# Evacuation order on ScalarE in two steps of nine, and a semaphore tie for the zeroing and the first weight loads, in an attention and routed-experts kernel

## The chip, the cores and the metric

The kernel runs on one core of one Trainium2 chip. The metric is the device time of one execution in microseconds (us). The kernel before was run three times: median 999.24 us, from 998.72 to 999.63. One further execution was profiled; every row quoted below is from that execution.

## What is computed

Attention over 8 batches of 8 heads, 576 positions of 64 values each, with a threshold: a score counts only where it lies within tau of its row's maximum. The output, 4608 rows of 512 values, goes through a layer of eight experts; each row goes to the one expert with the largest logit.

```python
scores = scale * np.matmul(q, k.transpose(0, 1, 3, 2))
thresh = np.max(scores, axis=-1, keepdims=True) - tau
scores = np.where(scores >= thresh, scores, -1000000000.0)
attn = np.exp(scores - np.max(scores, axis=-1, keepdims=True))
attn = attn / (np.sum(attn, axis=-1, keepdims=True) + 1e-09)
x = (attn @ v)                      # then (4608, 512)
logits = x @ w_gate
e_idx = np.argmax(logits, axis=1)
...
for e in range(E):
    mask = e_idx == e
    h = np.maximum(x[mask] @ w1[e], 0.0)
    out[mask] = gate_w[mask, None] * eom[mask, e, None] * (h @ w2[e])
```

## The kernel before

**Attention.** A unit `u` is one head of two batches; there are 32 units, taken two at a time: 16 pairs `m`. A pair has nine steps `s` (0 to 8), so the loop in `run` (L306) counts steps `g = 9 m + s` from 0 to 143. A step handles 128 query rows of both batches (step 4 of a pair takes the last 64 rows of both of its units). In a step, TensorE first writes the scores into the two `ps` tiles (L138). VectorE copies them out, negated and scaled, as `s`, with the row minimum in `mn` (L146). GpSimd adds tau: `thr` (L151). This instruction is kept as `router.gate`, so `gate` is always the threshold of the newest step. ScalarE takes the exponentials into `p` (L158, two instructions of 128x576). One step later VectorE sets to zero in `p` what misses the threshold and sums the rest (L171). Two steps later TensorE transposes `p` in 64x64 blocks into the tile `pt` (L213) and ScalarE copies `pt` into `PTa` or `PTb` (L216). There is one `pt` buffer, so the transposes of the next step wait for this copy. The product with v follows (L235, into `pa`), some of its matmuls in eight of the nine steps; `X` is its result (L240).

**Steps with rows.** In steps 1 and 5 of every pair from the second on (`ROWS`, L29), TensorE also turns the result of an earlier unit back into rows of x and multiplies them with the two gate matrices (L261). In these steps `p`'s remainder goes through the same two PSUM tiles (L197), and ScalarE copies `xl` (L327) and the remainder (L198) out of them. Then stand, on ScalarE, the exponentials of the step (L332) and behind them the copy of the blocks (L334, which calls `blocks`).

**A transfer on ScalarE's queue.** At the end of each odd unit, ScalarE issues a copy of `PTc` into `PTb` (L218), which L235 reads three steps later. As every transfer of the two hardware queues, it is given one of eight completion semaphores (lanes) in turn, whichever engine issues it, and before it is issued the engine waits until the earlier transfer of the same lane has landed.

**Routing.** From step 10 on, 32 transfers of 128 rows each (L446) write the same tile `zrow` to the buffer of routed rows `xs` in device memory; one is emitted per step. Later, rows of x are scattered into `xs` on GpSimd's queue (L461), with a wait for all 32 and for the gate of their step.

**Loads.** SyncE issues all other transfers: q and k of a unit (L92) and v (L97), two units ahead, and the experts' weights in pieces of 512 KB (L707 and L708). `begin` (L765) is called in step 129 and emits the first eight of these. For ScalarE, VectorE, TensorE and GpSimd the instructions stand in the order in which the program is written. SyncE's order is set by a scheduler: an instruction of SyncE is placed as early as the things that it depends on allow.

**Experts.** From about step 146 on, TensorE multiplies gathered rows with the weights (L927 to L929, L949 to L951), each number split into a high and a low part, and scaled rows are scattered into the output (L740).

Of the kernel before, what the change touches and what calls it, by code (L numbers as in the profile page):

```python
# [16 lines left out]
P = 128  # L17
# [3 lines left out]
class Attention:  # L21
# [279 lines left out]
    def run(self, hooks):  # L301
        nc, T, G, rt = self.nc, self.T, self.G, self.router
        W, NB = self.XW, self.NB
        st, pr, av, xls = {}, {}, {}, {}
        self.prep_first()
        for g in range(G + self.TAIL):  # L306
            m, s = divmod(g, T)
            if g < G:
                u, t = self.at(g)
                if t == 0 and u + 2 < self.nu:  # L310
                    self.load_qk(u + 2)
                    self.load_v(u + 2)
                st[g] = self.scores(u, t)
            if g in self.WARM:
                self.keep_warm(self.WARM[g])
            g2 = g - 2
            turn = 0 <= g2 < G
            if turn:
                dst = self.turned(*self.at(g2))
            xu = 2 * m + self.ROWS[s] if m and s in self.ROWS else None  # L320
            if xu is not None:
                ps = self.x_rows(xu)
                if turn:
                    out = self.remainder(dst, pr[g2], [x[:, 5 * W : 5 * W + 64] for x in ps])
                xl = xls[xu] = self.w2.tile([P, 2, 5, W], F32, name="xl")
                for a in (1, 0):
                    nc.scalar.copy(xl[:, a].rearrange("p j w -> p (j w)"), ps[a][:, 0 : 5 * W])  # L327
                    if turn:
                        out(a)
                self.x_out(xu, xl)  # L330
            if g < G:
                pr[g] = self.exps(u, t, *st[g])  # L332
            if turn and xu is not None:
                self.blocks(dst, pr.pop(g2))  # L334
            if s in self.AV:
                du, n = self.AV[s]
                au = 2 * m + du
                if 0 <= au < self.nu:
                    if au not in av:
                        av[au] = self.av_units(au)  # L340
                    for _ in range(n):
                        next(av[au])
            if turn and xu is None:
                p = pr.pop(g2)
                self.remainder(dst, p)
                u2, t2 = self.at(g2)
                self.blocks(dst, p, u2 % 2 and t2 == 2)
            if s in self.PLACE:
                rt.place(self.ps_r)
            g1 = g - 1  # L350
            if 0 <= g1 < G:
                self.masks(*self.at(g1), *st.pop(g1), pr[g1])
            lu = 2 * m + self.LOGITS[s] if m and s in self.LOGITS else None
            if g >= G:
                lu = xu
            if lu is not None and lu in xls:
                self.logits(lu, xls.pop(lu))
                if lu == self.nu - 1:
                    self.logit_sums(0)
                    self.logit_sums(1)  # L360
            if self.sumup and s in self.ROUTE:
                self.logit_sums(self.summed)
            if g in hooks:
                hooks[g]()
            rt.advance(s in self.ROUTE or m >= self.nu // 2 - 5)


class Router:
# [69 lines left out]
    def init_units(self):  # L438
        E = self.E
        parts = [(self.xs[self.A :, :], "itok")]  # L440
        for e in range(self.early, E + 1):
            n = self.base[e] if e < E else 2 * P
            parts.append((self.xs[e * self.CAP : e * self.CAP + n, :], "itok"))
        for dst, group in parts:
            for r in range(0, dst.shape[0], P):
                ins = self.nc.sync.dma_start(dst[r : r + P, :], self.zrow)  # L446
                self.nodep(ins, group)
                self.init.append(ins)
                yield False

# [216 lines left out]
class Experts:  # L667
# [26 lines left out]
        for name, bufs in (("y", 4), ("x", 2), ("h", 2)):  # L694
            setattr(self, f"ps_{name}", self.pool(f"ps_{name}", bufs, space=PSUM))

    def load(self, e, g):
        nc = self.nc
        r1 = self.raw.tile([P, 4, 256], F32, name="r1")
        r2 = self.raw.tile([P, 2, 512], F32, name="r2")  # L700
        cs = slice(g * 256, g * 256 + 256)
        if isinstance(e, int):
            s1, s2 = self.w1[e, :, cs], self.w2[e, cs, :]
        else:
            s1, s2 = self.w1[bass.ds(e, 1), :, cs], self.w2[bass.ds(e, 1), cs, :]
            s1, s2 = (s.rearrange("o d f -> (o d) f") for s in (s1, s2))
        nc.sync.dma_start(r1, s1.rearrange("(c p) f -> p c f", p=P))  # L707
        nc.sync.dma_start(r2, s2.rearrange("(c p) f -> p c f", p=P))  # L708
        return r1, r2

    def split_w(self, raw):
# [79 lines left out]
    def load_next(self):  # L791
        if self.nload < len(self.seq):
            i, g = self.seq[self.nload]
            self.nload += 1
            self.raws.append(self.load(self.unit(i).e, g))

    def split_until(self, n):
        while self.done < min(n, 2 * len(self.seq)):
# [345 lines left out]
```

## Time and profile before

| | |
|---|---|
| median of three runs | 999.24 us |
| the profiled execution, its own time | 1000.01 us |
| its span (first to last instruction) | 998.2 us |
| mean granted TensorE clock | 0.991 |
| busy TensorE, VectorE, ScalarE, GpSimd | 957.4, 691.0, 595.1, 347.2 us |
| moved by the transfer engines | 130.88 MB |

The span is 1.8 us shorter than the profiled execution's own time. The page cuts the span into 40 slices of 25 us; a digit is the busy share of a slice in tenths. In the list of waits, a row names the instruction that waited, then what released it, then microseconds in total, how often, and the longest. In a timeline, a row has the start, the duration, engine, line, what is written and read, and in brackets the idle time ahead of it with what ended it; rows that follow each other are merged, with their count. A row with `SPq` or `ACTq` is the issue of a transfer by that engine's queue, not the transfer.

### The profile page before, as it was taken

The numbers are of one execution on the slowest core, as the hardware profiler recorded it, in microseconds if no ns is written. First come the engines' busy times: TensorE is split into PE (matmuls) and PEld (weight loads), VectorE is DVE, ScalarE is ACT, GpSimd is POOL, SyncE is SP. The second block draws the span as 40 slices with busy tenths as digits, with TensorE's granted clock in tenths as the row PEclk, the third lists the DMA queues.
The fourth block names the chain that finished last, engine by engine and source line by source line (L and its number), as shares of the span: only waits on it lengthen the run. The fifth ranks groups of instructions, "written<-read, shape, count | busy, mean of one in ns | idle before, by whom it ended". The sixth has DMA issues, their size and how long they took to land. (4 is left out here: it accounts for less than half of the span.)

```text
span 998.2 us, 22132 instructions
## 1 busy us (share of the span) xinstructions
PE 957.4 (96%) x8491; PEld 715.0 (72%) x8491; DVE 691.0 (69%) x1632; ACT 595.1 (60%) x1052; POOL 347.2 (35%) x649
## 2 busy tenths in 40 slices
PE   9689999999999999999998999999999999999997
PEld 5456666666666666666667887788888878878785
DVE  7579989998899988998986675434634635535731
ACT  6478887877888778887884433333534424425621
POOL 4234343446844468454764821010102002002011
PEclk9799999999999999999999999999999999999999
DMA  9952222222432215223135775254644636527401
GB/s 270 309 176 87 75 67 88 59 73 58 158 95 58 88 51 164 86 64 86 61 98 180 243 244 179 86 168 127 202 154 142 215 100 209 182 85 234 157 21 44
DMA packets 87532, 130.88 MB, mean 131 GB/s; under 512 B 24831, under 2 KB 51711, under 8 KB 87424
## 3 DMA queue, kind: packets, MB, share of 16 engines
q1 hardware_dynamic: 62096, 103.70, 33.7%
q0 software_dynamic: 6640, 21.02, 5.5%
q10 hardware_dynamic: 18688, 4.72, 1.9%
q8 instruction: 68, 1.11, 0.5%
q14 instruction: 40, 0.33, 0.1%
HBM read 95.26 MB, written 30.22 MB: 126 GB/s over the span
## 5 line engine op out<-in xcount | busy, mean ns | idle before, releaser
L158 ACT ACTIVATE p<-s,mn 128x576 f32<-128x576 f32 x288 | 210.3, 783 | 65.4 <-DVE s L146 64.2
L146 DVE TENSOR_SCALAR_CACHE_REDUCE s<-ps 128x576 f32<-128x576 f32 x288 | 206.2, 753 | 43.1 <-PE ps L138 42.6
L171 DVE SCALAR_TENSOR_TENSOR p<-s,thr,p 128x576 f32<-128x576 f32 x288 | 224.8, 817 | 5.6 <-POOL thr L151 5.6
L138 PE MATMUL ps<-qk 64*128 64x288 f32 (+1 forms) x1280 | 182.6, 421 | 0.9 <-DVE s L146 0.6
L151 POOL TENSOR_SCALAR thr<-mn,tau_sb 128x2 f32<-128x2 f32 x144 | 99.4, 690 | 220.0 <-DVE s L146 217.9
L932 ACT ACTIVATE hh<-ph 128x512 fp32r<-128x512 f32 (+2 forms) x96 | 49.0, 511 | 201.9 <-PE ph L929 201.7
L740 POOL DMA_INDIRECT out_dram<-yo,kid x39 | 42.7, 1095 | 362.0 <-DVE yo L739 272.4
L933 DVE SCALAR_TENSOR_TENSOR hl<-ph,hh 128x512 fp32r<-128x512 f32 (+2 forms) x96 | 55.5, 578 | 136.6 <-ACT hh L932 136.6
L927 PE MATMUL ph<-xh,w1h 128*128 128x512 f32 (+2 forms) x384 | 135.9, 354 | 0.7 <-ACT xl L327 0.7
L928 PE MATMUL ph<-xl,w1h 128*128 128x512 f32 (+2 forms) x384 | 133.4, 347 | 0.2 <-DVE xl L752 0.2
L929 PE MATMUL ph<-xh,w1l 128*128 128x512 f32 (+2 forms) x384 | 133.2, 347 | 0.0
L138 PEld LDWEIGHTS ps<-qk 64*128 64x128 f32 (+1 forms) x1280 | 105.4, 178 | 27.3 <-DVE s L146 4.8
L951 PE MATMUL py<-w2h,hl 128*128 128x512 f32 x304 | 120.5, 396 | 1.2 <-DVE hl L933 1.2
L949 PE MATMUL py<-w2h,hh 128*128 128x512 f32 x304 | 120.2, 395 | 0.0
L950 PE MATMUL py<-w2l,hh 128*128 128x512 f32 x304 | 119.9, 394 | 0.0
L213 PE MATMUL pt<-ident,p 64*128 64x64 f32 x2304 | 101.2, 228 | 9.5 <-ACT PTb L216 9.5
L213 PEld LDWEIGHTS pt<-ident,p 64*128 64x128 f32 x2304 | 83.0, 138 | 30.3 <-issue 13.9
L235 PE MATMUL pa<-PTb,vld 128*64 128x320 f32 x640 | 101.1, 445 | 2.8 <-DMA PTb<-PTc 2.8
L235 PE MATMUL pa<-PTa,vld 128*64 128x256 f32 x640 | 83.9, 392 | 12.9 <-ACT PTb L198 12.9
L927 PEld LDWEIGHTS ph<-xh,w1h 128*128 128x128 f32 x384 | 72.1, 188 | 11.9 <-ACT xl L327 0.8
L928 PEld LDWEIGHTS ph<-xl,w1h 128*128 128x128 f32 x384 | 72.2, 188 | 10.2 <-DVE xl L752 0.6
L752 DVE TENSOR_TENSOR w1l<-r,w1h 128x1024 fp32r<-128x1024 f32 x52 | 64.0, 1230 | 21.5 <-ACT w1h L749 20.5
(203 smaller groups left out, 1501.3 us busy)
## 6 DMA issues: line engine op xcount, KB each, us to landing
r<-in_moe_w_dram SPq DMA_DIRECT2D x104, 512.0 KB, 3.9
qk<-in_qkv_dram SPq DMA_DIRECT2D x31, 608.0 KB, 4.1
vld<-in_qkv_dram SPq DMA_DIRECT2D x32, 320.0 KB, 4.0
xs<-zrow SPq DMA_DIRECT2D x32, 257.0 KB, 7.8
xg<-xs SPq DMA_DIRECT2D x6, 1028.0 KB, 5.4
PTb<-PTc ACTq DMA_DIRECT2D x16, 288.0 KB, 3.4
xg<-xs SPq DMA_DIRECT2D x4, 514.0 KB, 5.2
xg<-xs SPq DMA_DIRECT2D x2, 771.0 KB, 4.7
```

Source lines behind the costliest of these rows:

```text
L138: nc.tensor.matmul(ps[a][rows, o : o + HS], q[pp, t * P : t * P + w], k[pp, k0 : k0 + HS], start=True, stop=True)
L146: nc.vector.tensor_scalar(s, ps[a][:, c0 : c0 + S], SC, None, op0=ALU.mult, op1=ALU.min, accum_out=mn[:, a : a + 1])
L158: self.nc.scalar.activation(e, s, AF.Exp, bias=mn[:, a : a + 1], scale=-1.0)
L171: nc.vector.scalar_tensor_tensor(e, s, thr[:, a : a + 1], e, op0=ALU.is_le, op1=ALU.mult, accum_out=acc[:, a : a + 1])
L213: nc.tensor.transpose(pt[:, o : o + 64], p[hs[h], k0 : k0 + P], id_[hs[h], hs[h]])
L235: nc.tensor.matmul(pa[self.half[a], 0:N], vm[:, kb, a], PT[:, 4 * a + kb if i else self.NK - 1], start=(i == 0), stop=(i == self.NB), skip ...
L927: nc.tensor.matmul(ph, w1h[:, c, fs], self.xh[:, c, 0:N], start=(c == 0), stop=False)
L928: nc.tensor.matmul(ph, w1h[:, c, fs], self.xl[:, c, 0:N], start=False, stop=False)
L929: nc.tensor.matmul(ph, w1l[:, c, fs], self.xh[:, c, 0:N], start=False, stop=(c == 3))
L949: nc.tensor.matmul(Y, hh[:, ts], wh, start=(f == 0), stop=False)
L950: nc.tensor.matmul(Y, hh[:, ts], wl, start=False, stop=False)
L951: nc.tensor.matmul(Y, hl[:, ts], wh, start=False, stop=(f == 7))
```

## The change

Three edits. In `run`, the call of `blocks` in the steps with rows stands ahead of the exponentials. In `init_units`, each of the 32 zero writes waits for the threshold of the step that emits it. In `load`, the first eight weight loads wait for the threshold of the step that emits them, 129.

```diff
@@ run
                 self.x_out(xu, xl)
+            if turn and xu is not None:
+                self.blocks(dst, pr.pop(g2))
             if g < G:
                 pr[g] = self.exps(u, t, *st[g])
-            if turn and xu is not None:
-                self.blocks(dst, pr.pop(g2))
             if s in self.AV:
@@ init_units
                 ins = self.nc.sync.dma_start(dst[r : r + P, :], self.zrow)
                 self.nodep(ins, group)
+                self.after(ins, [self.gate])
                 self.init.append(ins)
@@ Experts.load
-    def load(self, e, g):
+    def load(self, e, g, gate=None):
...
-        nc.sync.dma_start(r1, s1.rearrange("(c p) f -> p c f", p=P))
-        nc.sync.dma_start(r2, s2.rearrange("(c p) f -> p c f", p=P))
+        for r, s in ((r1, s1), (r2, s2)):
+            ins = nc.sync.dma_start(r, s.rearrange("(c p) f -> p c f", p=P))
+            if gate is not None:
+                self.rt.after(ins, [gate])
         return r1, r2
@@ load_next
-            self.raws.append(self.load(self.unit(i).e, g))
+            self.raws.append(self.load(self.unit(i).e, g, self.rt.gate if self.nload <= self.RB else None))
```

On TensorE, VectorE and GpSimd no instruction moves. On ScalarE two rows change places in each step with rows. This is ScalarE's order in steps 1 and 2 of the second pair, before:

```order
L327 COPY xl<-pa 128x400
L198 COPY PTb<-pa 128x64
L327 COPY xl<-pr 128x400
L198 COPY PTb<-pr 128x64
L158 ACTIVATE p<-s,mn 128x576 x2
L216 COPY PTb<-pt 128x8x128
L158 ACTIVATE p<-s,mn 128x576 x2
```

and now:

```order
L327 COPY xl<-pa 128x400
L198 COPY PTb<-pa 128x64
L327 COPY xl<-pr 128x400
L198 COPY PTb<-pr 128x64
L216 COPY PTb<-pt 128x8x128
L158 ACTIVATE p<-s,mn 128x576 x4
L240 COPY X_206<-pa 128x256
```

The copy of `pt` has moved ahead of the step's two exponentials, which now stand directly ahead of those of the next step. The 30 steps with rows of the pairs from the second on all change in this way.

SyncE's queue near the start of the program, before (`qk_406` belongs to unit 3, `qk_595` and `vld_597` to unit 4; `r1_7321` and `r2_7322` are the first weights):

```order
L97 DMA vld_408<-in_qkv_dram 128x640
L446 DMA xs_71<-zrow_139 128x514 x9
L92 DMA qk_406<-in_qkv_dram 128x1216
L446 DMA xs_71<-zrow_139 128x514 x17
L92 DMA qk_595<-in_qkv_dram 128x1216
L446 DMA xs_71<-zrow_139 128x514 x5
L97 DMA vld_597<-in_qkv_dram 128x640
L446 DMA xs_71<-zrow_139 128x514
L707 DMA r1_7321<-in_moe_w1_dram 128x4x256
L708 DMA r2_7322<-in_moe_w2_dram 128x2x512
```

and now (`qk_868` and `vld_870` belong to unit 5, `qk_1081` to unit 6):

```order
L97 DMA vld_408<-in_qkv_dram 128x640
L92 DMA qk_406<-in_qkv_dram 128x1216
L92 DMA qk_595<-in_qkv_dram 128x1216
L97 DMA vld_597<-in_qkv_dram 128x640
L446 DMA xs_71<-zrow_139 128x514 x3
L92 DMA qk_868<-in_qkv_dram 128x1216
L446 DMA xs_71<-zrow_139 128x514
L97 DMA vld_870<-in_qkv_dram 128x640
L446 DMA xs_71<-zrow_139 128x514 x3
L92 DMA qk_1081<-in_qkv_dram 128x1216
L446 DMA xs_71<-zrow_139 128x514 x2
```

The zero writes now stand in groups of one to three between the loads of units 4 to 12, and every one of them waits for its own step. The first `PTc` copy of ScalarE gets another lane by this: before, its lane was last used by the 27th zero write (the first of the group of five above); now by the load of unit 1's q and k at the program's start.

SyncE's queue at the end of attention, before, held the loads of the last units (`qk_7393` and `vld_7395` are unit 31's) with nothing between them:

```order
L92 DMA qk_7081<-in_qkv_dram 128x1216
L97 DMA vld_7083<-in_qkv_dram 128x640
L92 DMA qk_7393<-in_qkv_dram 128x1216
L97 DMA vld_7395<-in_qkv_dram 128x640
L892 DMA xg_8127<-xs_71 128x3x514
```

and now (line numbers of the changed kernel, in which L709 is the weight load):

```order
L92 DMA qk_7081<-in_qkv_dram 128x1216
L97 DMA vld_7083<-in_qkv_dram 128x640
L709 DMA r1_7321<-in_moe_w1_dram 128x4x256
L709 DMA r2_7322<-in_moe_w2_dram 128x2x512
L709 DMA r1_7325<-in_moe_w1_dram 128x4x256
L709 DMA r2_7326<-in_moe_w2_dram 128x2x512
L709 DMA r1_7329<-in_moe_w1_dram 128x4x256
L709 DMA r2_7330<-in_moe_w2_dram 128x2x512
L709 DMA r1_7333<-in_moe_w1_dram 128x4x256
L709 DMA r2_7334<-in_moe_w2_dram 128x2x512
L92 DMA qk_7393<-in_qkv_dram 128x1216
L97 DMA vld_7395<-in_qkv_dram 128x640
```

The eight weight loads, 4 MB, have moved past the loads of 26 units and stand ahead of the last unit's.

## The prediction

> **What bounds the kernel now.** I read the page first: busy time by engine and in 40 slices.
>
> ```profile
> span 998.2 us, 22132 instructions
> PE 957.4 (96%) x8491; PEld 715.0 (72%) x8491; DVE 691.0 (69%) x1632; ACT 595.1 (60%) x1052; POOL 347.2 (35%) x649
> PE   9689999999999999999998999999999999999997
> PEclk9799999999999999999999999999999999999999
> DMA  9952222222432215223135775254644636527401
> ```
>
> TensorE (PE) is busy 96% of the span and in nearly every slice; it sets the end. It idles 998.2 - 957.4 = 40.8 us. Only the second and third slice (25 to 75 us) break the row: busy falls to 6 and 8 tenths, the granted clock to 7 in the second, just where the transfer engines are full. The list of waits says what TensorE stands for:
>
> ```profile
> PE pa L235 <- ACT PTb L198: 12.9, 16, 8.5
> PE pt L213 <- ACT PTb L216: 9.5, 15, 0.6
> PE pa L235 <- DMA PTb<-PTc: 2.8, 1, 2.8
> PE pr L526 <- ACT PTa L205: 1.3, 3, 0.5
> ```
>
> So there are two different things: one hole of 8.5 us with a smaller one of 2.8, and a wait of 0.6 us that comes back 15 times, once for each of the 15 pairs that have steps with rows. The rest of the first row, 12.9 - 8.5 = 4.4 us, is a wait for the remainder's copy (L198), which the change leaves in front as it was.
>
> **The hole.** TensorE's timeline around it, with the next two pairs (an L197 row marks step 1 of a pair at 35.94, 81.14 and 111.94):
>
> ```profile
> 35.94 0.22 PE L197 MATMUL pr<-ident,p 64*128 64x64 f32 x1
> 45.19 1.97 PE L235 MATMUL pa<-PTa,vld 128*64 128x256 f32 x8 [8.54 <-ACT PTb L198]
> 55.30 2.11 PE L235 MATMUL pa<-PTb,vld 128*64 128x320 f32 x8 [2.81 <-DMA PTb<-PTc]
> 81.14 0.22 PE L197 MATMUL pr<-ident,p 64*128 64x64 f32 x1
> 82.11 1.08 PE L235 MATMUL pa<-PTa,vld 128*64 128x256 f32 x8 [0.26 <-ACT PTb L198]
> 111.94 0.22 PE L197 MATMUL pr<-ident,p 64*128 64x64 f32 x1
> 118.44 1.30 PE L235 MATMUL pa<-PTb,vld 128*64 128x320 f32 x8
> ```
>
> ScalarE and its queue at the same time, then SyncE's queue, then the landing times:
>
> ```profile
> 43.81 0.68 ACTq L218 DMA_DIRECT2D PTb<-PTc  x1
> 44.53 0.49 ACT L327 COPY xl<-pa 128x400 f32<-128x400 f32 x1 [9.47 <-DMA xs<-zrow]
> 110.11 0.60 ACTq L218 DMA_DIRECT2D PTb<-PTc  x1
> ```
>
> ```profile
> 35.45 4.75 SPq L446 DMA_DIRECT2D xs<-zrow  x5
> 42.23 0.43 SPq L707 DMA_DIRECT2D r<-in_moe_w_dram  x1
> 50.24 2.12 SPq L708 DMA_DIRECT2D r<-in_moe_w_dram  x1
> ```
>
> ```profile
> xs<-zrow SPq DMA_DIRECT2D x32, 257.0 KB, 7.8
> PTb<-PTc ACTq DMA_DIRECT2D x16, 288.0 KB, 3.4
> qk<-in_qkv_dram SPq DMA_DIRECT2D x31, 608.0 KB, 4.1
> ```
>
> ScalarE had nothing to wait for from TensorE, yet stood 9.47 us, and a zero write ended that. Ahead of L327 on its queue is the issue of the `PTc` copy, which must wait for its lane. The lane's last user is the first zero write issued at 35.45; with the median landing of 7.8 it is done at 43.25, and the issue follows at 43.81. Behind the issue stand the copies that free `pa`, and so TensorE stands. Then the `PTc` copy itself travels among the last zero writes and the weight loads of 42 to 52 us: it is used 55.30 - 43.81 = 11.5 us after its issue, against a median landing of 3.4. That is the second hole.
>
> **Part one: zero writes and weights move away.** The interval from step 1 to step 1 is 81.14 - 35.94 = 45.20 us with the holes and 111.94 - 81.14 = 30.80 without. The difference, 14.40, is 8.54 + 2.81 of idle and 3.05 of slower matmuls behind them: eight L235 took 1.97 instead of 1.08, and 2.11 instead of 1.30.
>
> By the Trainium skill ("TensorE: Matmul & The Clock Gate", section "What's actually happening") the array falls to half its clock only after an idle window of about 3.4 us and is back after as long of work. An estimate from that page gives 8.54 + 2.81 + 1.7 = 13.05, since a gap of 2.81 would cost no clock; the 2.11 behind that gap speaks against it here.
>
> I take 14.4. The `PTc` copy's lane was now last used by a load from the first microseconds, so its issue does not wait. Where do the moved transfers collide now? The zero writes come one in a step, behind `thr`. On SyncE's queue the loads of q, k and v stand behind them, and whoever reads those waits on TensorE. Two rows show the spare time; 90.94 is unit 7's load and 120.52 the first scores that read it:
>
> ```profile
> 90.94 0.33 SPq L92 DMA_DIRECT2D qk<-in_qkv_dram  x1
> 120.52 1.20 PE L138 MATMUL ps<-qk 64*64 64x288 f32 x16
> 469.88 0.33 SPq L92 DMA_DIRECT2D qk<-in_qkv_dram  x1
> 499.58 0.71 PE L138 MATMUL ps<-qk 64*64 64x288 f32 x8
> ```
>
> 120.52 - 90.94 - 4.1 = 25.5 us to spare; a gate holds a load back by a step at most (30.80 / 9 = 3.4). The eight weight loads took about 10 us (42.23 to 52.36) and now stand ahead of unit 31's loads, which have 499.58 - 469.88 - 4.1 = 25.6 us to spare. Both cost nothing; without that cover, a weight burst ahead of a load costs its 10 us once. In GpSimd's queue nothing moves; the scatters are emitted after the last zero write, as before.
>
> **Part two: the copy ahead of the exponentials.** Steps 5 and 6 of an ordinary pair on ScalarE, TensorE and VectorE:
>
> ```profile
> 96.77 1.47 ACT L158 ACTIVATE p<-s,mn 128x576 f32<-128x576 f32 x2
> 98.12 1.03 ACT L216 COPY PTb<-pt 128x1024 f32<-128x1024 f32 x1
> 99.01 1.48 ACT L158 ACTIVATE p<-s,mn 128x576 f32<-128x576 f32 x2
> ```
>
> ```profile
> 98.17 0.39 PE L202 MATMUL pr<-ident,p 128*64 128x128 f32 x4
> 99.20 0.71 PE L213 MATMUL pt<-ident,p 64*128 64x64 f32 x16 [0.64 <-ACT PTb L216]
> 99.74 1.19 PE L138 MATMUL ps<-qk 64*128 64x288 f32 x8
> ```
>
> ```profile
> 98.12 0.75 DVE L146 TENSOR_SCALAR_CACHE_REDUCE s<-ps 128x576 f32<-128x576 f32 x1
> 98.80 0.81 DVE L171 SCALAR_TENSOR_TENSOR p<-s,thr,p 128x576 f32<-128x576 f32 x1
> 99.54 0.87 DVE L171 SCALAR_TENSOR_TENSOR p<-s,thr,p 128x576 f32<-128x576 f32 x1
> 100.97 0.76 DVE L146 TENSOR_SCALAR_CACHE_REDUCE s<-ps 128x576 f32<-128x576 f32 x1 [0.55 <-PE ps L138]
> 446.27 0.76 DVE L146 TENSOR_SCALAR_CACHE_REDUCE s<-ps 128x576 f32<-128x576 f32 x1 [0.34 <-PE ps L138]
> ```
>
> TensorE could go on at 98.17 + 0.39 = 98.56 but `pt` is being copied until 99.15. With the copy first, from 96.77 to 97.80, `pt` is free 0.76 before that: the 0.64 goes, 15 times, 9.5 us. The other 15 steps with rows (step 1) show no wait for `pt`, so there the edit brings nothing. The price is an exponential that ends 1.03 later. VectorE masks it in the next step: the first half would be ready at 96.77 + 0.74 + 1.03 = 98.54, and is taken at 98.80; the second at 98.24 + 1.03 = 99.27, taken at 99.54. So 0.26 is left in both and the price is nothing; were it not, it would be up to 1.03 a step. ScalarE's next exponentials, at 99.01, come after the same sum of work and do not move.
>
> What is late next? Step 7's scores need `ps`, free at 98.12 + 0.75 = 98.87; they would start at 99.74 - 0.64 = 99.10. VectorE waits for them 0.55 in an ordinary pair, so it can take the 0.64 nearly whole. In a pair in which routing is placed (the L526 row: three) it waited only 0.34, so about 0.3 is lost there, 0.9 in all. I take 9.5 - 0.9 = 8.6.
>
> **Sum.** 14.4 + 8.6 = 23.0, from the profiled execution's 1000.01: 977.0. The median of the runs, 999.24, is 0.8 lower, so for a median: 976.2. Bounds: part one from 11.35 (idle alone) to 14.4, part two from nothing to 9.5 and the 1.3 of the L526 row.
>
> **Rivals.**
>
> *VectorE takes part two back.* With 691.0 us it is the busiest engine after TensorE; if it is the next to be late in every pair, 999.24 - 14.4 = 984.8. Against it: the 0.55 it idles at 100.97. Chance 0.12.
>
> *The strewn zero writes delay the later `PTc` copies.* In the three pairs that follow they share the engines with zero writes. The copy of 110.11 is used at 118.44, 8.3 later; if it took the 11.5 of the crowd, 3.2 a pair, 9.6 in all: 985.8. Against it: one zero write in a step, where the 32 now follow each other. Chance 0.05. The Trainium skill ("DMA: Bandwidth & Descriptors", section "Issuing engines are not separate DMA queues") says that a copy issued by ScalarE interleaves with SyncE's on the same engines, so its own queue is no shelter; 11.5 against 3.4 agrees.
>
> *The lane was not the cause*, or another wait takes its place at the same spot: only part two is left, 999.24 - 8.6 = 990.6. Chance 0.04.
>
> *Slower: the late exponential.* If the 0.26 that VectorE has to spare is used up in the steps with rows, each of the 30 shows up to its 1.03, 30.9 in all, and the 9.5 is not gained: 999.24 - 14.4 + 30.9 = 1015.7. It decides from an exponential that ends over 0.26 later than worked out. Chance 0.03.
>
> *Nothing to measure*: the ends cancel. Chance 0.01.
>
> **How the numbers follow.** The forecast has 0.75. Its low end is 999.24 - 14.4 - 9.5 - 1.3 = 974.0, with 0.5 for the spread of the runs 973.5. Upwards the range takes in its own bounds and the first rival: 985.0. That leaves the other rivals (0.13) and tails of the forecast (about 0.05) outside. A difference under 0.2% (2 us) can't be told from none. Faster: 0.75 + 0.12 + 0.05 + 0.04 = 0.96; same 0.01; slower 0.03.
>
> **What would show it.** Right: the list of waits has no L235 row above 1 us, no L213 row for `PTb`; the `PTc` copy of the second pair is issued near 35 and no ScalarE row is ended by a zero write; the clock row has no 7 in the second slice; zero writes appear about one in 3.4 us from 37 us on; an ordinary pair takes 30.80 - 0.64 = 30.2 us. Wrong: a new VectorE row under TensorE's waits or a pair of 30.8 (first rival), L235 waiting for `PTb<-PTc` in pairs 3 to 5 (second), VectorE's L171 waiting for L158 (the slower one).

## The result and the profile after

| | before | after |
|---|---|---|
| median (4 runs each) | 998.98 us (997.88 to 999.63) | 980.20 us (979.83 to 981.19) |
| the profiled execution, its own time | 1000.01 us | 979.83 us |
| its span | 998.2 us | 978.1 us |
| mean granted TensorE clock | 0.991 | 0.998 |

The ratio is 0.9813 (95% interval 0.9800 to 0.9826). The gain is 18.8 us between the medians and 20.2 us between the two profiled executions; 23.0 was forecast. 980.2 lies in the range, 4.0 above the predicted 976.2. So most of the account holds, and some 3 us of it are missing. The rest of this document is about which.

The page of the kernel after, its rows on the span, the busy time and the slices:

```profile
span 978.1 us, 22170 instructions
PE 956.6 (98%) x8491; PEld 714.0 (73%) x8491; DVE 689.9 (71%) x1632; ACT 592.9 (61%) x1052; POOL 345.5 (35%) x649
PE   9999999999999999999989999999999999999997
PEclk9999999999999999999999999999999999999999
DMA  4355453122422225135246874345636526536401
```

The dip in the second and third slice is gone, and with it the 7 in the clock row. The transfer engines, at 9, 9 and 5 tenths in the first three slices before, are at 4, 3 and 5. TensorE's idle time fell from 40.8 to 978.1 - 956.6 = 21.5 us. Its busy time is nearly the same (957.4 and 956.6).

TensorE's rows in the list of waits after (microseconds in total, times, longest):

```profile
PE pa L235 <- ACT PTb L198: 4.6, 16, 0.7
...
PE pr L202 <- DVE p L171: 1.1, 4, 0.3
...
PE pa L235 <- DMA PTb<-PTc: 0.2, 1, 0.2
```

The wait of 8.5 is gone from the first row. The row of 9.5 for `pt` (L213) is gone altogether. The row of 2.8 for `PTc` is down to a single 0.2, in the last pair. But there is a row that before did not have: L202 waits for VectorE's L171, four times. It is small, two waits each in pairs 6 and 10, and it is the track of what is missing.

ScalarE and SyncE's queue at the place of the hole, after:

```profile
34.22 0.68 ACTq L218 DMA_DIRECT2D PTb<-PTc  x1
36.32 0.49 ACT L327 COPY xl<-pa 128x400 f32<-128x400 f32 x1 [1.14 <-PE pa L197]
```

```profile
37.53 7.75 SPq L446 DMA_DIRECT2D xs<-zrow  x3
48.22 0.33 SPq L446 DMA_DIRECT2D xs<-zrow  x1
51.82 6.06 SPq L446 DMA_DIRECT2D xs<-zrow  x3
```

The copy is issued at 34.22, right behind the copy of `pt`, and what ends L327's idle time is TensorE (1.14) and no transfer. The zero writes come one in a step: three from 37.53 to 45.28. TensorE in the same stretch, and step 1 of the next two pairs:

```profile
36.05 0.22 PE L197 MATMUL pr<-ident,p 64*128 64x64 f32 x1
36.98 1.08 PE L235 MATMUL pa<-PTa,vld 128*64 128x256 f32 x8 [0.21 <-ACT PTb L198]
42.49 1.30 PE L235 MATMUL pa<-PTb,vld 128*64 128x320 f32 x8
66.10 0.22 PE L197 MATMUL pr<-ident,p 64*128 64x64 f32 x1
96.20 0.22 PE L197 MATMUL pr<-ident,p 64*128 64x64 f32 x1
```

The two groups of eight L235 take 1.08 and 1.30 where they took 1.97 and 2.11. An ordinary pair takes 96.20 - 66.10 = 30.10 us.

**Where the time went.** L197 stands at the start of steps 1 and 5, so its rows cut attention into intervals that can be compared one by one. Their differences, pairs counted as the code's `m`:

| interval | before | after | gain |
|---|---|---|---|
| step 1 to step 5 of pair 1 (the hole) | 28.73 | 14.29 | 14.44 |
| step 1 to step 5 of the other pairs, each | 14.33 to 14.34 (16.11 in pair 14) | the same within 0.02 | 0.0 |
| step 5 to step 1, pairs 1, 2, 3 | 16.47 or 16.48 | 15.76 | 0.71 or 0.72 each |
| pairs 4, 5, 8, 9, 12, 13 | 16.84, 17.28, 16.83, 17.29, 16.84, 17.54 | 16.19, 16.65, 16.19, 16.65, 16.18, 17.02 | 0.65, 0.63, 0.64, 0.64, 0.66, 0.52 |
| pairs 6, 7, 10, 11, 14, 15 | 17.99, 16.78, 18.00, 16.78, 16.58, 14.54 | 17.96, 16.76, 17.96, 16.76, 16.57, 14.52 | 0.01 to 0.04 each |

From the first L197 to the last it is 483.94 before and 463.51 after: 20.43, of which 14.44 is the hole and 5.99 is all else. The span fell by 20.1, since the first L197 comes 0.11 later and the stretch behind the last one (478.32 and 478.54) is 0.22 longer. So part one came out as forecast (14.4), and part two brought 6.0 in place of 8.6. It did not bring a little less in each pair: it brought 0.52 to 0.72 in nine pairs and next to nothing in the others.

**Why not in pair 6.** VectorE's row for L171 in the list of waits and its row in pair 6, before and then after:

```profile
DVE p L171 <- POOL thr L151: 5.6, 5, 1.6
...
228.43 0.88 DVE L171 SCALAR_TENSOR_TENSOR p<-s,thr,p 128x576 f32<-128x576 f32 x1 [1.60 <-POOL thr L151]
```

```profile
DVE p L171 <- POOL thr L151: 8.7, 5, 2.2
...
210.67 0.88 DVE L171 SCALAR_TENSOR_TENSOR p<-s,thr,p 128x576 f32<-128x576 f32 x1 [2.21 <-POOL thr L151]
```

In five pairs (6, 7, 10, 11 and 15) VectorE waited already before for the threshold that GpSimd makes. Now it gets there 0.6 earlier and waits 0.6 longer: 8.7 - 5.6 = 3.1, which is 5 x 0.62. GpSimd's timeline in pair 6 after, from the threshold of step 5 to that of step 6:

```profile
202.82 0.79 POOL L151 TENSOR_SCALAR thr<-mn,tau_sb 128x2 f32<-128x2 f32 x1 [2.81 <-DVE s L146]
203.58 1.67 POOL L274 TENSOR_TENSOR rows<-xl,rinv 128x256 f32<-128x256 f32 x2
205.23 1.38 POOL L276 TENSOR_SCALAR rows<-xl,rinv 64x64 f32<-64x64 f32 x2
...
207.94 2.42 POOL L542 TENSOR_TENSOR bs<-pr,bs 128x8 f32<-128x8 f32 x9
210.34 0.29 POOL L151 TENSOR_SCALAR thr<-mn,tau_sb 128x2 f32<-128x2 f32 x1
```

From 202.82 on GpSimd hardly idles. In this step it makes the rows of x (1.67 and 1.38), and then nine small additions of routing, 2.42 us, stand ahead of the threshold. VectorE's L171 starts 0.04 behind that threshold's end, and TensorE's L202 waits for both halves of L171:

```profile
211.70 0.40 PE L202 MATMUL pr<-ident,p 128*64 128x128 f32 x2 [0.23 <-DVE p L171]
212.42 0.43 PE L202 MATMUL pr<-ident,p 128*64 128x128 f32 x2 [0.31 <-DVE p L171]
```

So the 0.65 is lost. In pairs 7, 11 and 15 a scatter (L462, issue 1.06) stands at the place of the additions. There TensorE shows no idle time for it: the loss stands in the length of its own rows. In pair 7, L202 takes 0.62 for 0.39 and the eight scores behind it 1.91, where they took 1.49 before.

### The profile page after: what moved, and what is told of

The parts are those of the page before. It is cut to its first block, busy times and chain, and to the rows that moved or that the text cites. A ratio compares the mean times of both kernels' runs of the same rounds, so it can differ in the third digit from the quotient of the medians.

```text
span 978.1 us, 22170 instructions
## 1 busy us (share of the span) xinstructions
PE 956.6 (98%) x8491; PEld 714.0 (73%) x8491; DVE 689.9 (71%) x1632; ACT 592.9 (61%) x1052; POOL 345.5 (35%) x649
## 5 line engine op out<-in xcount | busy, mean ns | idle before, releaser
L158 ACT ACTIVATE p<-s,mn 128x576 f32<-128x576 f32 x288 | 209.0, 790 | 59.3 <-DVE s L146 59.1
L171 DVE SCALAR_TENSOR_TENSOR p<-s,thr,p 128x576 f32<-128x576 f32 x288 | 224.7, 817 | 8.7 <-POOL thr L151 8.7
L213 PE MATMUL pt<-ident,p 64*128 64x64 f32 x2304 | 100.7, 227 | 0.0
L235 PE MATMUL pa<-PTb,vld 128*64 128x320 f32 x640 | 100.3, 442 | 0.2 <-DMA PTb<-PTc 0.2
L213 PEld LDWEIGHTS pt<-ident,p 64*128 64x128 f32 x2304 | 82.6, 138 | 19.6 <-issue 11.8
L235 PE MATMUL pa<-PTa,vld 128*64 128x256 f32 x640 | 83.0, 389 | 4.6 <-ACT PTb L198 4.6
L755 DVE TENSOR_TENSOR w1l<-r,w1h 128x1024 fp32r<-128x1024 f32 x52 | 64.0, 1231 | 21.5 <-ACT w1h L752 20.7
```

The lines of the kernel that those rows point to most:

```text
L158: self.nc.scalar.activation(e, s, AF.Exp, bias=mn[:, a : a + 1], scale=-1.0)
L171: nc.vector.scalar_tensor_tensor(e, s, thr[:, a : a + 1], e, op0=ALU.is_le, op1=ALU.mult, accum_out=acc[:, a : a + 1])
L213: nc.tensor.transpose(pt[:, o : o + 64], p[hs[h], k0 : k0 + P], id_[hs[h], hs[h]])
L235: nc.tensor.matmul(pa[self.half[a], 0:N], vm[:, kb, a], PT[:, 4 * a + kb if i else self.NK - 1], start=(i == 0), stop=(i == self.NB), skip ...
```

## The experiments

Theory A is that of the prediction: the hole is ScalarE's wait for the lane of a zero write in front of its own issue, and the rest follows from it. Theory B, for the missing part: GpSimd's routing work in step 5 sets the end there, and no order on ScalarE can help. Rivals: the crowd on the transfer engines itself made the hole (to A), and VectorE, busy as it is, takes the rest (to B). Runs e1 to e4 were compared with 17 runs of the kernel before on the same chip (median 1001.33, 998.58 to 1004.75), e5 to e7 with 9 on another (1000.56, 998.30 to 1003.04). The expectations reckon from 999.0, so it is their gains that can be compared, not their end times.

### e1: the order alone

```diff
+            if turn and xu is not None:
+                self.blocks(dst, pr.pop(g2))
             if g < G:
                 pr[g] = self.exps(u, t, *st[g])
-            if turn and xu is not None:
-                self.blocks(dst, pr.pop(g2))
```

> The kernel before with only the copy of pt ahead of the exponentials. Theory now, from the trace of the changed kernel: the 0.64 us is kept in nine of the fifteen pairs (1 to 5, 8, 9, 12, 13 by m), since in the other six GpSimd's routing work makes the threshold of step 6 late and eats it: 9 x 0.64 = 5.8, so about 993.2 against 999.0. Forecast as it stood: 8.6, so 990.4. Rival that VectorE takes all of it back: 999.0. The hole near 36 us stays: an ACT row ended by a zero write, 8 to 9 us of TensorE's idle.

Measured 993.92, ratio 0.9929 (0.9908 to 0.9951): 7.4 us less, interval 4.9 to 9.2. Every interval from step 5 to step 1 agrees with that of the kernel after within 0.01, the hole stays. ScalarE's and TensorE's rows at it:

```profile
44.91 0.49 ACT L327 COPY xl<-pa 128x400 f32<-128x400 f32 x1 [8.82 <-DMA xs<-zrow]
```

```profile
45.57 1.98 PE L235 MATMUL pa<-PTa,vld 128*64 128x256 f32 x8 [7.88 <-ACT PTb L198]
54.78 1.30 PE L235 MATMUL pa<-PTb,vld 128*64 128x320 f32 x8 [0.95 <-DMA PTb<-PTc]
```

So the order is worth 6.0 by the intervals, without help from the ties. It also shows that the hole is not of one size: in this execution it cost 25.64 - 14.29 = 11.4 from step 1 to step 5 where the profile of before has 14.4, and the second gap, 0.95 here, left no slow matmuls behind it.

### e2 and e3: both ties, and the zero writes' tie alone

e2 has the old order and both ties. e3 is e2 without the weights' tie:

```diff
-            self.raws.append(self.load(self.unit(i).e, g, self.rt.gate if self.nload <= self.RB else None))
+            self.raws.append(self.load(self.unit(i).e, g, None))
```

> The kernel before with both ties (zero writes and first weight loads) and the old order on ScalarE. Theory: the hole and the slow matmuls behind it go, 14.5 us in the profiles (45.20 to 30.7 between two L197 rows of step 1), so about 984.5 to 985.5 against 999.0; all fifteen L213 waits of 0.6 us stay. Rival that the two edits only pay together: over 990.

> Only the zero writes are tied; the weights load as early as SyncE can, and old order on ScalarE. In the built program the lane of the first PTc copy was then last used by one of the first weight loads, which stand ahead of unit 3's q and k. Lane theory: no wait of the issue, no hole, the same as with both ties, 984.5 to 985.5. Rival that the 4 MB of weights in the first 36 us are themselves what crowds the transfers: a hole of several us at the start or at the PTc copy, over 988.

Measured 988.10 for each: e2 0.9874 (0.9853 to 0.9895), e3 0.9875 (0.9853 to 0.9897), so 13.2 us less with an interval of 10.5 to 14.7 for e2. In both the hole's interval is 14.29, and the 15 waits for `pt` stay. TensorE's two first waits in e3:

```profile
PE pt L213 <- ACT PTb L216: 9.5, 15, 0.7
PE pa L235 <- ACT PTb L198: 4.6, 16, 0.7
```

The zero writes' tie does all of part one. The weights' tie adds nothing that can be measured. The gain of 13.2 is under the 13.5 to 14.5 that was expected, but the interval takes them in; the 988.10 of e3 is no sign of its rival, since its profile shows no hole.

### e4: the weights' tie alone

The zero writes stay untied, the first eight weight loads wait for step 129 as in the change.

> Only the first weight loads are tied; the zero writes run as before, and old order on ScalarE. In the built program the lane of the first PTc copy was last used by unit 4's load of q and k, issued about 1 us ahead of the zero write that ended the wait before. Lane theory: the hole stays within 2 us of its 8.5 and the row of ScalarE's wait names qk instead of xs<-zrow; the second hole (2.8) goes, since the PTc copy no longer travels among weights: 3 to 6 us gained, 993 to 996. Rival that the zero writes as such held ScalarE: the row still names xs<-zrow.

Measured 996.76, ratio 0.9958 (0.9945 to 0.9971): 4.6 us less, interval 2.9 to 5.5. ScalarE at the hole, and SyncE's queue ahead of it:

```profile
34.49 1.02 ACT L216 COPY PTb<-pt 128x1024 f32<-128x1024 f32 x1
41.72 0.68 ACTq L218 DMA_DIRECT2D PTb<-PTc  x1
42.44 0.49 ACT L327 COPY xl<-pa 128x400 f32<-128x400 f32 x1 [6.94 <-DMA qk<-in_qkv_dram]
```

```profile
34.67 0.34 SPq L92 DMA_DIRECT2D qk<-in_qkv_dram  x1
```

The hole is there, 6.0 for TensorE's L235 (the interval from step 1 to step 5 is 21.59, 7.3 over that with the ties), and what ends ScalarE's idle time is now a load of q and k, which a copy of `xl` does not read. With another order of transfers the copy shares its lane with another transfer, and waits for that one. The second gap is gone: with no weight loads behind it, the `PTc` copy of 41.72 was in time. The size of the first hole was to stay within 2 of 8.5, and 6.0 misses that narrowly, since the load issued at 34.67 was through earlier than the zero write.

### e7: the first copy of `PTc` issued by GpSimd

Everything of before stays in the source, the crowd too; only who issues the first copy changes.

```diff
-                nc.scalar.dma_start(self.PTb[:, :, self.QA :], self.PTc)
+                (nc.scalar if self.tc_done else nc.gpsimd).dma_start(self.PTb[:, :, self.QA :], self.PTc)
+                self.tc_done = True
```

> The kernel before with the first PTc copy alone issued by GpSimd, whose transfers have completion semaphores of their own; nothing else changes. Lane theory: ScalarE no longer stands in front of L327, and TensorE's 8 us for L198 go; the copy now starts at 35 to 37 us amid zero writes, needs up to 11.5 us and is used at about 42.5, so a wait of 1 to 5 us for PTb takes its place: 4 to 9 us faster than before. Rival, the crowd of transfers itself slows ScalarE: the wait for L198 stays at 6 to 8 us.

Measured 990.85 (987.50 to 993.00, four runs), ratio 0.9909 (0.9887 to 0.9930): 9.7 us less. GpSimd's row, then SyncE's queue, then TensorE (the edit shifts L235 to L237 and L198 to L199):

```profile
33.82 1.23 POOL L219 DMA_DIRECT2D PTb<-PTc  x1
```

```profile
29.96 3.79 SPq L448 DMA_DIRECT2D xs<-zrow  x5
...
35.11 5.24 SPq L448 DMA_DIRECT2D xs<-zrow  x5
```

```profile
36.85 1.08 PE L237 MATMUL pa<-PTa,vld 128*64 128x256 f32 x8 [0.20 <-ACT PTb L199]
42.76 1.30 PE L237 MATMUL pa<-PTb,vld 128*64 128x320 f32 x8 [0.32 <-ACT PTa L217]
```

The zero writes are as thick as before, and the hole is gone: the interval is 14.66, 0.37 more than with the ties. So in this execution the crowd alone makes no hole; ScalarE's stand in front of its own issue does. This settles theory A against its rival. The wait of 1 to 5 us for `PTb` that was expected in its place is 0.32 at most: that is what the second row has, put down to a copy into `PTa` that these matmuls do not read. The Trainium skill ("DMA: Bandwidth & Descriptors", section "Anatomy of one DMA — SWDGE (gpsimd) path") says that a semaphore wait of a DMA is done by the sequencer that issues it, before dispatch; e4's 6.94 and e7's missing wait agree.

The profiled execution of e7 took 987.50 and is the fastest of the four; the others took 990.15 to 993.00. By the medians e7 brings 9.7 (7.0 to 11.3), where the ties brought 13.2 on the other chip. Why its runs vary is not shown; a `PTc` copy that lands late in the crowd would do it, but only the fastest run has a trace.

### e5 and e6: no routing work in step 5

e5 is the kernel after with this edit, e6 the kernel with both ties and the old order with the same edit.

```diff
-            rt.advance(s in self.ROUTE or m >= self.nu // 2 - 5)
+            if s != 5 or m >= 13:
+                rt.advance(s in self.ROUTE or m >= self.nu // 2 - 5)
```

Routing work, the zero writes among it, is then not emitted in step 5 of pairs up to 12 and comes in the steps behind it. Up to pair 10 the code lets only those routing pieces through in step 5 that need no VectorE (`ROUTE`, L32, does not have 5), so what the edit takes out of step 5 there is none of VectorE's work. From pair 13 on it stays, since the first gather needs all scatters.

> The changed kernel in which the routing does not advance in step 5 of the pairs up to m = 12, so that GpSimd's nine additions (L541) or a scatter (L461) of that step come a step later, when GpSimd has no rows of x to write. Theory that GpSimd makes the threshold of step 6 late in pairs 6, 7, 10 and 11: from step 5 to the next step 1 those pairs take 17.96, 16.76, 17.96, 16.76 us in the changed kernel and come down to 15.8 to 16.6, together 3 to 6 us less than the changed kernel. Rival that VectorE's own work is the bound there: the same intervals, no gain.

> The same edit of the routing with both ties and the old order on ScalarE. GpSimd theory: the order edit is worth 0.65 to 0.7 in thirteen pairs instead of nine, so this kernel is 8 to 9 us slower than the changed kernel with the same edit (against 6.0 without it), and pairs 6, 7, 10 and 11 show L213's wait of 0.6 as all others do. Rival, VectorE is the bound: the distance stays at 6.0.

Measured: e5 975.66, ratio 0.9753 (0.9736 to 0.9771), the shortest of all kernels here. e6 983.97, ratio 0.9839 (0.9822 to 0.9857). GpSimd in pair 6 of e5:

```profile
203.21 0.79 POOL L151 TENSOR_SCALAR thr<-mn,tau_sb 128x2 f32<-128x2 f32 x1 [2.81 <-DVE s L146]
203.97 1.67 POOL L274 TENSOR_TENSOR rows<-xl,rinv 128x256 f32<-128x256 f32 x2
...
208.08 0.29 POOL L151 TENSOR_SCALAR thr<-mn,tau_sb 128x2 f32<-128x2 f32 x1
208.32 0.19 POOL L541 COPY bs<-cnt 128x8 f32<-128x8 f32 x1
208.59 3.45 POOL L543 TENSOR_TENSOR bs<-pr,bs 128x8 f32<-128x8 f32 x9
```

VectorE's row in the list of waits of e5:

```profile
DVE p L171 <- POOL thr L151: 1.9, 3, 1.4
```

The nine additions stand behind the threshold of step 6 now. It ends 208.37 - 203.21 = 5.16 after step 5's began, in place of 210.63 - 202.82 = 7.81. The wait falls from 8.7 to 1.9, and the row of L202 waiting for L171 is gone. Pairs 6, 7, 10 and 11 take 15.76 each from step 5 to step 1, as pairs 1 to 3 do; in e6, with the old order, 16.46 to 16.48. So with the routing work out of the way the order is worth its 0.7 in these pairs too. From the first L197 to the last it is 465.87 in e6 and 457.13 in e5: 8.74 for the order edit, where the prediction had 8.6 and the change itself got 5.99. The measured difference is 983.97 - 975.66 = 8.3. The routing edit alone shortens these four pairs by 69.55 - 65.88 = 3.7 with the old order (before against e6), and by 69.44 - 63.04 = 6.4 with the new one, a little over the 3 to 6 expected. VectorE's rival falls for these pairs: VectorE does the same work as before, and it keeps up as soon as the threshold is early.

## Why the prediction was right or wrong

**Part one was right, mechanism and size.** 14.40 was forecast and 14.44 found between the two profiles. e3, e4 and e7 show the cause that the prediction only inferred from the rows: the lane. The rival that it was not the lane (990.6) is out. The split of the 14.40 was a little off: an ordinary pair idles too (0.26 at the same L235), so it is 11.1 of idle time and 3.3 of slower matmuls (TensorE's busy time is 33.22 and 29.90 in the two intervals). The prediction's estimate by the Trainium skill ("TensorE: Matmul & The Clock Gate", section "What's actually happening"), 13.05, is 1.4 short of the 14.44. It had no cost of clock for the gap of 2.81, but the trace of before has a granted clock of 0.58 from 55.3 to 57.3 us and 0.50 from there to 59.0, behind that gap, and that of e1 has 1.00 behind its gap of 0.95. These slow matmuls are gone in the trace of after (1.30 for 2.11). Measured by runs, part one is 13.2 (10.5 to 14.7); the interval takes in the 14.4, and a hole that varies, as e1's 11.4 has it, would bring the median down, which is not shown.

**The covers held.** The weights' move cost nothing (e2 against e3). The strewn zero writes delayed no copy of pairs 3 to 5: no row of L235 waits for `PTc` there, and the median landing of a zero write fell from 7.8 to 3.4. That rival (985.8) is out. So is the late exponential (1015.7): no row of L171 waits for L158, and the stretch from step 5 to step 1 became shorter in nine pairs and longer in none.

**The mis-sized term is the give-back in part two.** The part of the prediction that missed is "What is late next?", with its end "about 0.3 is lost there, 0.9 in all. I take 9.5 - 0.9 = 8.6". All 15 waits of L213 went, 9.5 us, as forecast, but 3.5 came back, and at another place than priced. The three pairs in which routing is placed on TensorE (5, 9 and 13) were to lose 0.3 each; they kept 0.63, 0.64 and 0.52. The pairs that lost all were 6, 7, 10, 11, 14 and 15. I had asked whether VectorE could follow in step 7 and found 0.55 of idle time in an ordinary pair. I had not asked whether VectorE itself waits for the threshold of step 6, though the profile of before already showed L171 waiting for GpSimd's threshold, five times, 5.6 us in total. A wait that is there before the edit is a place with no slack: what arrives earlier there waits longer. Five pairs x 0.62 are 3.1 by that row, and pair 14 is another 0.6: 3.7 lost, against which pairs 1 to 3 gained 0.2 more than 0.64.

**Pair 14** has no such row, yet lost all. VectorE and TensorE there after, and TensorE's same scores before:

```profile
460.18 0.17 DVE L570 TENSOR_TENSOR dsti<-dst,off 128x9 int32<-128x9 f32 x1 [1.13 <-POOL off L568]
```

```profile
461.11 1.91 PE L138 MATMUL ps<-qk 64*128 64x288 f32 x8
```

```profile
482.02 1.30 PE L138 MATMUL ps<-qk 64*128 64x288 f32 x8
```

TensorE's weight loads (PEld) for the scores in this stretch, 454.12 to 470.69, after, as one group with what ended their idle time:

```profile
L138 PEld LDWEIGHTS ps<-qk 64*128 64x128 f32 x40 | 4.0, 187 | 0.9 <-DVE s L146 0.4
```

The eight scores of step 7 start earlier, but take 1.91 for 1.30. The 0.61 is the wait of L213 at another place. TensorE waits among them for `ps` (0.4 in the last row), which VectorE empties late, since ahead of that copy it waits 1.13 for GpSimd's `off`, a piece of routing. Before the change VectorE waited 1.13 for `off` at the same place, so this too could be read in advance. It is GpSimd again, by another instruction. For this pair and for pair 15 (1.42 for L171, 0.78 before) that is read from the rows and not shown, since no run took the routing work out of them. The first rival (984.8), VectorE as the next to be late in every pair, was wrong in nine pairs; in the other six VectorE was late because it had waited for GpSimd.

**The list of what would show it.** Every point of "right" came out: no wait of L235 above 1 us (the longest is 0.7), no L213 row, the copy at 34.22, no 7 in the clock, a zero write in about 3.4 us, an ordinary pair of 30.10 for 30.2. The point of "wrong" that named a new VectorE row under TensorE's waits came out as well, with four waits. The sum by the intervals is 14.44 + 5.99 = 20.43 for 23.0, and in the median 18.8. Of the 1.6 between the two, some 0.2 lie outside the intervals and 1.4 are spread: the profiled execution of before is 1.03 above its median, that of after 0.37 below.

**The range.** It was to take in the prediction's own bounds upwards, but idle time alone for part one and nothing for part two give 999.24 - 11.35 = 987.9, above the 985.0. The result lies well below both, so nothing hung on this.

## What to carry to other kernels

An issue of a transfer on a compute engine's queue can hold up everything behind it; when an engine idles and a transfer that it doesn't read ended that, look at what shares a completion semaphore with the transfer issued there. When a wait is taken away, walk on to the next engines step by step and look for waits that stand there already: each such row is a place where the gain will end. A wait on one engine that is off the bound (here GpSimd, busy 35%) can eat a gain in just those stretches where its small work stands ahead of the one instruction that others need.

## What the runs showed that I had not expected

- The hole is not a fixed price: 14.4 us in the profile of before, 11.4 in that of e1, with the same order of transfers in SyncE's queue.
- The stretch behind the last L197, almost all of it the experts, that no edit here was aimed at, took 478.3 us (before), 478.5 (after), 479.8 (e7), 479.9 (e6), 480.2 (e3), 480.3 (e4, e5), 480.8 (e1) and 481.1 (e2) in the profiles. In the list of waits, one row of TensorE in that stretch differs with it: the wait for VectorE's `hl` is 1.2 us in total before and after, and 2.2 to 2.9 in the other seven. Those seven ran on other occasions, on two chips, so whether the chip, the execution or the kernel makes the difference is not shown. But 2 to 3 us between two profiles can come from there alone, and an edit of 6 us is better read from intervals than from end to end.
- Nine additions of 128x8 took 2.42 us on GpSimd in the kernel after and 3.45 in e5, a step later and with a row of `thr` behind them as before. VectorE stood idle during most of them in the kernel after and worked through them in e5; that this is the reason is not shown.
